# Another place for a block's attention steps in the first tile of a fused attention and two-layer network kernel

## The chip, the cores and the metric

The kernel runs on one core of a Trainium2 chip. The metric is the device time of one execution, in microseconds. Before the change it is 1495.19 us (median of 3 runs, 1493.69 to 1496.91). The execution that was profiled took 1492.79 us; its span in the trace is 1491.0 us.

## The reference

Attention is computed in chunks of 64 positions (softmax of 0.125 * q k^T over 64 keys, times v) for 8 batches, 8 heads and 576 positions, head size 64. Its output is reshaped to 4608 tokens of 512 numbers. Then come two networks:

```
attn = softmax(0.125 * q_c @ k_c.T)          # per chunk of 64, rows divided by (sum + 1e-9)
x = (attn @ v_c) as 4608 x 512
h = x @ w_in                                 # 512 -> 2048
x = (h * cos(h)) @ w_out                     # 2048 -> 512
y = ((x @ w1) * (x @ w2)) @ w3 @ moe2_w_out  # 512 -> 1024, 1024 -> 1024, 1024 -> 512
```

All is in float32. On TensorE each operand is split into a high part and a low part, and each product is made of three matmuls (`mm3`: high*high on L107, high*low on L108, low*high on L109).

## The kernel before

The 4608 tokens are worked in 9 tiles of 512 tokens. A tile's attention is done in 4 blocks of 128 tokens. The first network runs in two passes over the tiles. The first pass does groups 0 to 4 of the 8 groups into which w_in and w_out are cut, the second does groups 5 to 7. The change is in the first pass over tile 0, that is, in the first five groups (i = 0 to 4), which are the only ones that use the strings `ORDER0` (groups 0 to 3) and `ORDER0E` (group 4).

The work is written out by hand: the loop at L823 walks the string of its group letter by letter, and each letter emits instructions at the end of the queues of the engines. Every engine then works through its own queue in that order. What the letters do in these groups:

- `P` and `Q`: the **first product** and the **second product** of the group, each two blocks of 12 matmuls of 256 columns into one of two PSUM buffers (`bank_h`). The first block needs the group's first w_in part in W, the second block the second one. A buffer comes free when `B` (for P) or `D` (for Q) of the group before has read it.
- `s`: the product of the group before is split into high (ScalarE, L598) and low (GpSimd, L599) parts, two instructions each.
- `x` and `y`: the first and the second half of the **output product** of the group before (24 matmuls of 512 columns in all).
- `a`, `A`, `b`, `B` and `c`, `C`, `d`, `D`: the chain from h to h * cos(h) for P and for Q. The small letter is ScalarE's (L576, then the sine at L586), the capital one VectorE's (L581, then the product at L590).
- `v`: one step of the conversion of the weights (`conv_tick`, L189); there are four in a group, called **steps 1 to 4** here. A step does its part for three weights at once. On ScalarE: L183 (high part), L130, and L206 for w_out. On VectorE: L138, L131, L132, and L209 (low part) for w_in. For w_out the low part is added by a transfer that GpSimd issues (L207, w<-cw). Steps 1 and 2 finish the two w_out parts of the group; steps 3 and 4 finish the two w_in parts of the next group.
- `q`: the next attention step of the group's block, in the order **scores** (L386 on TensorE, then two maxima and two subtractions on VectorE, L395 and L397, and the loads of a coming q and k block), **exponential** (ScalarE, L403), **scale** (sums and reciprocals on VectorE, L408 to L411, then a multiplication on GpSimd, L412), **transposes** (TensorE, L419, then a copy on ScalarE, L422) and **values** (TensorE, L433, two copies on ScalarE, L438, and the load of the next v block).

Sine and exponential are in different ScalarE tables, so an `ACT_TABLE_LOAD` stands before the one that follows the other.

In a group before the change the scores stand between P and Q, the exponential behind Q and step 2, the scale behind C, the transposes behind D, and the values at the very end. Block 4 + n is done within group n, for n = 0 to 3. Group 4 has no attention steps. It splits tile 1's input (`o`, L477: a high part on ScalarE and a low part on VectorE, four times), which group 5's first product needs.

Of the kernel before, what the change touches and what calls it, by code (L numbers as in the profile page):

```python
# [34 lines left out]
START = "A0 A1 B0 x B1 E0 A2 C0 B2 E1 A3 D0 C1 x B3 D1 E2 o o E3 C2 D2 x C3 D3 x o o"  # L35
NE = 4

ORDER0 = "PsvaAqQvqcCqxybBdvDqvq"
ORDER0E = "PsvaAQvcCxybBodDoooL"
ORDER1P = "PsqMhQqqHaclAxqbCrRmBdyqDL"  # L40
ORDER1PE = "SPsQacATCoobBoxodoDyoo"
ORDER1 = "1s2qMh5qqHa3clAxqbCrRmBdyqDL"
# [15 lines left out]
def chunk_attention_two_ffn(  # L58
# [38 lines left out]
    def f32(ap):  # L97
        return ap.bitcast(F32)
# [119 lines left out]
    def sum_load(g):  # L218
        pair = ("in", g)
        loaded.append((g, pair, new_w((pair, 2))))  # L220
        nc.sync.dma_start(out=f32(W[pair, 2]), in_=wr[g])
# [23 lines left out]
    def need(*keys):  # L245
        while not all(key in W for key in keys):
            assert (pump() if cat[3] == len(cq) else conv_tick()), keys
# [4 lines left out]
    def st_load():  # L252
        while sat[0] < min(len(sq), sat[2] + 2):
            load_w(sq[sat[0]])
            sat[0] += 1
# [40 lines left out]
    def st_hi():  # L296
        for _, x, hi, lo in now.get("parts", ()):
            nc.scalar.activation(hi.bitcast(F32R), x, AF.Copy)
# [143 lines left out]
    def att_tok(step, early):  # L442
        (att_scores, att_softmax, att_scale, att_transpose, att_values)["ABECD".index(step[0])](int(step[1:]), early)
# [144 lines left out]
    def chain_g(i, h, which):  # L588
        t = rr[i, which]
        nc.vector.tensor_tensor(out=t, in0=t, in1=h, op=ALU.mult)  # L590

    def split_g(i):

        gg[i] = t = one.tile([P, 8, 256], F32R, tag="g", name="g")
        for which in range(2):
            r = rr.pop((i, which)).rearrange("p (i t) -> p i t", i=2)
            hi, lo = (t[:, 2 * s + which:2 * s + which + (6, 4)[which]:(5, 3)[which]] for s in range(2))
            nc.scalar.activation(hi, r, AF.Copy)  # L598
            nc.gpsimd.tensor_tensor(out=lo, in0=r, in1=f32(hi), op=ALU.subtract)  # L599
# [44 lines left out]
    def load_w3():  # L644
        key = ("w3", n3[0])
        n3[0] += 1
        if key in staged:
            W[key] = t = wk.tile([P, 2, TT], F32R, tag="qk", name="w3")
            nc.sync.dma_start(out=f32(t), in_=staged.pop(key))
# [134 lines left out]
    with tc.manual_schedule():  # L784
# [22 lines left out]
        def order_of(i, nth, end):  # L807
            if i < GA:
                return ORDER0E if end else ORDER0
            if i < 2 * GA:  # L810
                return ORDER1PE if end else ORDER1P
            if i <= iA:
                return ORDER1E if end else ORDER1
            if i < iB:
                return ORDER2
            return (ORDER3X if nxt in xs else ORDER3E) if end else ORDER3B if nth else ORDER3
# [3 lines left out]
        iA, iB = (NTILE - 1) * GA, NTILE * GA  # L820
        n_sums = 0
        fq = 0
        for i in range(NG):  # L823
            if i == GA:
                sq.extend(("wo2", j) for j in range(FB2))
                for g in range(GA, G1):
                    sq.extend((nm, 2 * g + e) for nm in ("in", "out") for e in range(2))
                    lq.extend((("in", g), p_) for p_ in range(4))
                    lq.extend(("out", 2 * g + e) for e in range(2))
                lq.extend(("wo2", j) for j in range(FB2))  # L830
                sq.extend(("w3", j) for j in range(N3))
                for f in range(FB2):
                    sq.extend((nm, f) for nm in ("w1", "w2"))
                    if N3 + f < 16:
                        sq.append(("w3", N3 + f))
                lq.extend((("w12", u), p_) for u in range(UNITS) for p_ in range(4))
                st_load()
            if i == iB + FOLD - 1:
                load_w3()
                load_w3()  # L840
            ps, n, g = groups[i]
            k_tile = (i - iB) // (G1 - GA)
            nxt = PASS2[k_tile + 1] if 0 <= k_tile < NTILE - 1 else None
            nth = (g, g - GA)[ps]
            end = g == (GA, G1)[ps] - 1

            def load_x(op):
                if op in pre:
                    X[op], pre[op] = pre[op], X[op]
                else:  # L850
                    nc.sync.dma_start(out=f32(X[op]), in_=xs[nxt][op])

            need(*((("in", g), p_) for p_ in range(2 if i < 2 * GA else 4)))
            z = Plain(("in", g)) if i < 2 * GA else Seven(
                ("in", g), (bank_h,) * 4, False, load_x if ps and end and nxt in xs else None)
            if i:
                need(*(("out", 2 * groups[i - 1][2] + e) for e in range(2)))
            n_q = n_o = 0
            for op in order_of(i, nth, end):
                if op == "s" and i:  # L860
                    split_g(i - 1)
                elif op == "x" and i:
                    x2_mm(i - 1, 0)
                elif op == "y" and i:
                    x2_mm(i - 1, 1)
                elif op == "v":
                    conv_tick()
                elif op == "L":
                    if n_sums < GA:
                        sum_load(n_sums)  # L870
                        n_sums += 1
                elif op == "M":
                    if loaded and i > GA + loaded[0][0]:
                        sum_make()
                elif op in "HR":
                    if sp:
                        {"H": sum_hi, "R": sum_lo}[op]()
                elif op == "l":
                    st_low()
                elif op == "m":  # L880
                    st_bits()
                elif op == "h":
                    st_hi()
                elif op == "r":
                    st_lo()
                elif op in "1253PQ":
                    getattr(z, "step" + op)()
                elif op in "ac":
                    chain_t(i, z.d if op == "a" else z.e, "ac".index(op))
                elif op in "AC":  # L890
                    chain_r(i, z.d if op == "A" else z.e, "AC".index(op))
                elif op in "bd":
                    chain_cos(i, "bd".index(op))
                elif op in "BD":
                    chain_g(i, z.d if op == "B" else z.e, "BD".index(op))
                elif op == "q":
                    if i < iA and nth < 4:
                        att_tok(steps[20 * n + 5 * nth + n_q], False)
                    elif i >= iB + FOLD and fq < 4 * FB2:
                        need(("w3", fq // 2), *(("wo2", j) for j in range(FB2)))  # L900
                        fold(fq // 4, fq % 4)
                        fq += 1
                        if fq == 4 * FB2:
                            load_wf(0)
                            load_wf(1)
                    n_q += 1
                elif op in "ST":
                    x_sums("ST".index(op))
                elif op == "o":
                    if i < GA and not n_o:  # L910
                        x_plain()
                    x_op((z.done if i < GA or i >= 2 * GA else OPS)[n_o], n + 1 if ps == 0 else None)
                    n_o += 1
            if i >= iA:
                pump()
            if n == (NTILE - 1, PASS2[-1])[ps]:
                done_with((("in", g), p_) for p_ in range(4))
            if ps == 1:
                if nth == 0 and nxt in xs:
                    if not pre:  # L920
                        xr = one.tile([P, CC, TT], F32R, tag="xf", name="xr")
                        pre.update((op, xr[:, 2 * j:2 * j + 2]) for j, op in enumerate(("B11", "B21")))
                    for op in pre:
                        nc.sync.dma_start(out=f32(pre[op]), in_=xs[nxt][op])
                if nth == 0 and nxt not in xs:
                    if pre:
                        pre.clear()
                        xf = one.tile([P, CC, TT], F32, tag="xf", name="xf")
                    nc.sync.dma_start(out=xf, in_=x2d[ALONE] if nxt is None else xd[nxt])
                if end:  # L930
                    for c in range(CC):
                        load_x2a(n, c)
# [119 lines left out]
```

## Time and profile before

| | before |
|---|---|
| median of 3 runs | 1495.19 us |
| profiled execution / its span | 1492.79 / 1491.0 us |
| TensorE matmul busy | 1447.5 us, 97% |
| VectorE busy | 1089.2 us, 73% |
| ScalarE busy | 692.0 us, 46% |
| GpSimd busy | 272.7 us, 18% |

The busy shares are means over all stages. The span is cut in 40 slices of 37.3 us on the page: TensorE is busy for 6 and 7 tenths in the first two and for nine or more in nearly all others. The first tile lies between 27.6 and 108.6 us. A view of busy times by stretch gives for each stretch its length and the busy time of TensorE's matmuls (PE), its weight loads (PEld), VectorE (DVE), ScalarE (ACT) and GpSimd (POOL), each with its count of instructions, and the granted TensorE clock as a share of 2.4 GHz. The stretches below begin and end where a group's first product ends: in groups 0, 1, 2, 3 and 4 at 32.9, 50.4, 69.6, 84.1 and 100.4 us; at 108.6 us the first product of group 5 begins. A row of a timeline tells when an instruction started, how long it took, its engine, line and operands, and in brackets how long its engine had been idle and what released it. A count such as x2 means that as many neighbours were merged. An instruction can start before the row ahead of it has ended, since the engines overlap the end of one with the start of the next.

### The profile page before, as it was taken

To read this page: it belongs to the slowest core of one execution; us is meant where nothing else is said; L and a number is where in the kernel's file an instruction comes from. 1 tells how busy PE (TensorE), PEld (TensorE's weight loads), DVE (VectorE), ACT (ScalarE), POOL (GpSimd) and SP (SyncE) were. 2 spreads that over 40 slices of the span, in tenths; PEclk is the share of its full clock that TensorE was granted. 3 is DMA by queue.
4 is the path that set the end of the run, shared out by engine and by line. 5 is a ranking of instruction groups with operands and counts; after the bars stand their busy time and mean duration, and the time that the engine had idled before them with its cause. 6 is when DMAs were issued, how large, how long until landed. Compare 5 with 4: busy or idle time off the path is not lost.

```text
span 1491.0 us, 26050 instructions
## 1 busy us (share of the span) xinstructions
PE 1447.5 (97%) x9996; PEld 1251.0 (84%) x9996; DVE 1089.2 (73%) x1834; ACT 692.0 (46%) x1183; POOL 272.7 (18%) x204
## 2 busy tenths in 40 slices
PE   6799999999999999999999999999999999999998
PEld 5688888888888889988888889998888888888887
DVE  7886788898888887777777777676565666656553
ACT  4776677787776775444444444231032023014002
POOL 0332222222222222221122222122000100200000
PEclk9899999999999999999999999999999999999999
DMA  8784656575664718998889784586435442641611
GB/s 270 216 243 143 217 174 217 163 244 192 220 226 139 247 65 297 372 335 323 303 309 333 241 294 148 193 332 247 148 113 192 169 148 96 234 150 58 212 35 57
DMA packets 124252, 310.00 MB, mean 208 GB/s; under 512 B 13792, under 2 KB 25824, under 8 KB 122976
## 3 DMA queue, kind: packets, MB, share of 16 engines
q1 hardware_dynamic: 122688, 305.71, 58.9%
q0 software_dynamic: 1440, 2.62, 1.0%
q8 instruction: 79, 1.29, 0.4%
q14 instruction: 45, 0.37, 0.1%
HBM read 210.50 MB, written 95.16 MB: 205 GB/s over the span
## 4 chain that ended last, share of the span: by engine, by line
PE 77%; DVE 10%; ACT 5%; DMA 3%; issue 2%; POOL 2%; SPq 0%; DVEq 0%; ACTq 0%; POOLq 0%
PE acc L107 11%; PE acc L108 11%; PE acc L109 10%; PE ps_hh L107 10%; PE ps_hh L109 10%; PE ps_hh L108 10%; PE ps_aa L107 5%; PE ps_aa L108 5%; PE ps_aa L109 5%; ACT L403 2%; POOL ex L412 1%; DMA w<-cw 1%; DVE sm L408 1%; PE ps_at L419 1%; PE ps_v L433 1%
## 5 line engine op out<-in xcount | busy, mean ns | idle before, releaser
L599 POOL TENSOR_TENSOR g<-t,g 128x512 fp32r<-128x512 f32 x144 | 198.4, 1398 | 559.2 <-ACT g L598 504.7
L107 PE MATMUL acc<-g,w 128*128 128x512 f32 x576 | 228.6, 397 | 0.0
L108 PE MATMUL acc<-g,w 128*128 128x512 f32 x576 | 226.1, 392 | 0.0
L109 PE MATMUL acc<-g,w 128*128 128x512 f32 x576 | 225.0, 391 | 0.0
L109 PE MATMUL ps_hh<-T,w 128*128 128x256 f32 (+1 forms) x616 | 182.5, 296 | 5.0 <-DVE w L209 5.0
L107 PE MATMUL ps_hh<-T,w 128*128 128x256 f32 (+1 forms) x616 | 185.2, 301 | 0.0
L108 PE MATMUL ps_hh<-T,w 128*128 128x256 f32 (+1 forms) x616 | 182.0, 295 | 0.0
L109 PEld LDWEIGHTS acc<-g,w 128*128 128x128 f32 x576 | 108.6, 189 | 23.6
L109 PEld LDWEIGHTS ps_hh<-T,w 128*128 128x128 f32 x616 | 118.8, 193 | 8.1 <-DVE w L209 5.6
L108 PEld LDWEIGHTS acc<-g,w 128*128 128x128 f32 x576 | 109.0, 189 | 19.8 <-POOL g L599 0.6
L107 PEld LDWEIGHTS acc<-g,w 128*128 128x128 f32 x576 | 109.0, 189 | 19.8
L107 PE MATMUL ps_hh<-B,w 128*128 128x256 f32 (+1 forms) x396 | 120.6, 304 | 4.0 <-DVE t L590 2.6
L107 PEld LDWEIGHTS ps_hh<-T,w 128*128 128x128 f32 x616 | 118.7, 193 | 5.4
L108 PEld LDWEIGHTS ps_hh<-T,w 128*128 128x128 f32 x616 | 118.8, 193 | 3.2
L109 PE MATMUL ps_hh<-B,w 128*128 128x256 f32 (+1 forms) x396 | 116.9, 295 | 0.2 <-DVE w L209 0.2
L108 PE MATMUL ps_hh<-B,w 128*128 128x256 f32 (+1 forms) x396 | 116.9, 295 | 0.0
L773 ACT ACTIVATE phl<-e 128x512 fp32r<-128x512 f32 x32 | 20.3, 633 | 202.0 <-DVE e L771 202.0
L586 ACT ACTIVATE t<-t,half_pi 128x512 f32<-128x512 f32 x144 | 98.4, 716 | 1.4
L107 PE MATMUL acc<-wf,phl 128*128 128x512 f32 x252 | 98.2, 390 | 0.0
L108 PE MATMUL acc<-wf,phl 128*128 128x512 f32 x252 | 98.1, 389 | 0.0
L109 PE MATMUL acc<-wf,phl 128*128 128x512 f32 x252 | 98.0, 389 | 0.0
L576 ACT ACTIVATE t<-d 128x512 int32<-128x512 f32 x62 | 38.9, 627 | 121.3 <-DVE d L530 121.3
(211 smaller groups left out, 3431.5 us busy)
## 6 DMA issues: line engine op xcount, KB each, us to landing
w<-sd SPq DMA_DIRECT2D x159, 512.0 KB, 6.0
sd<-raw SPq DMA_DIRECT2D x104, 256.0 KB, 4.5
s<-sd SPq DMA_DIRECT2D x43, 256.0 KB, 5.1
qk<-in_q_dram SPq DMA_DIRECT2D x36, 256.0 KB, 4.5
qk<-in_k_dram SPq DMA_DIRECT2D x36, 256.0 KB, 4.6
x2a<-x2o SPq DMA_DIRECT2D x36, 256.0 KB, 3.1
x2a<-x2a SPq DMA_DIRECT2D x36, 256.0 KB, 5.6
x2d<-x2a SPq DMA_DIRECT2D x36, 256.0 KB, 3.1
```

The costliest lines, as they stand in the source:

```text
L107: nc.tensor.matmul(ps, a[0], b[0], start=first, stop=False)
L108: nc.tensor.matmul(ps, a[0], b[1], start=False, stop=False)
L109: nc.tensor.matmul(ps, a[1], b[0], start=False, stop=last)
L403: nc.scalar.activation(ex, ex, AF.Exp, scale=SCALE)
L408: nc.vector.reduce_sum(out=sm, in_=ex, axis=AX.X)
L412: (nc.vector if early else nc.gpsimd).tensor_tensor(out=ex, in0=ex, in1=rc.unsqueeze(2).to_broadcast([P, 2 * HP, 64]), op=ALU.mult)
L419: nc.tensor.transpose(ps[:, P * h:P * h + P], ex[:, 2 * h:2 * h + 2].rearrange("p e k -> p (e k)"), ident)
L433: nc.tensor.matmul(ps[c][64 * e:64 * e + 64, h], vt[r, e, h], pt[r, h, o:o + 64], start=True, stop=True)
L576: nc.scalar.activation(t.bitcast(I32), h, AF.Copy, scale=INV2PI, bias=0.25)
L586: nc.scalar.activation(t, t, AF.Sin, scale=TWO_PI, bias=half_pi)
L599: nc.gpsimd.tensor_tensor(out=lo, in0=r, in1=f32(hi), op=ALU.subtract)
L773: nc.scalar.activation(t[:, 0], e0, AF.Copy)
```

## The change

The four `q` of `ORDER0` go, and digits take their places: 6 scores, 7 exponential, 8 scale, 9 transposes, 0 values. The digits 6, 7 and 8 work on the group's own block, 9 and 0 on the block of the group before, so that they do nothing in group 0. Group 4 gets 9 and 0 for the last block of the tile.

```
-ORDER0 = "PsvaAqQvqcCqxybBdvDqvq"
-ORDER0E = "PsvaAQvcCxybBodDoooL"
+ORDER0 = "PsvaA9Qv0cCx6ybBd7vD8v"
+ORDER0E = "PsvaA9Qv0cCxybBodDoooL"
...
+        at_first = {c: NE for c in "67890"}
...
+                elif op in "67890":
+                    if i or op in "678":
+                        att_tok("ABECD"["67890".index(op)] + str(at_first[op]), False)
+                        at_first[op] += 1
```

So the transposes stand between P and Q (where the scores stood), the values behind Q and step 2, the scores between x and y, the exponential behind the second sine (`d`), and the scale between D and step 4.

## Rows read from the trace of the kernel before

**Rows 1.** Busy times by stretch: from:to, us, five engines, clock, DMA share, GB/s
```profile
32.90:50.40 17.50, 11.46 (x121) 10.31 (x120) 14.80 (x25) 12.06 (x21) 5.83 (x5) 0.71 0.72 212
50.40:69.60 19.20, 15.06 (x145) 13.04 (x145) 15.57 (x26) 13.23 (x22) 5.65 (x5) 0.93 0.83 222
69.60:84.10 14.50, 13.81 (x145) 12.30 (x144) 12.92 (x24) 12.82 (x22) 3.50 (x3) 0.97 0.77 244
84.10:100.40 16.30, 13.86 (x144) 12.27 (x144) 16.09 (x25) 12.92 (x23) 7.99 (x8) 1.00 0.82 242
100.40:108.60 8.20, 8.20 (x50) 7.24 (x49) 5.07 (x9) 5.53 (x10) 1.18 (x2) 1.00 1.02 287
108.60:1491.00 1382.40, 1366.24 (x9117) 1179.76 (x9115) 1001.06 (x1675) 619.88 (x1057) 246.91 (x176) 1.00 0.59 205
```

**Rows 2.** Timeline of TensorE, groups 0 to 2
```profile
42.07 1.12 PE L419 MATMUL ps_at<-ident,ex 128*128 128x128 f32 x4 [5.35 <-POOL ex L412]
...
48.27 0.58 PE L109 MATMUL ps_hh<-T,w 128*128 128x256 f32 x1
...
50.37 0.69 PE L386 MATMUL ps_s<-qk 64*64 64x64 f32 x32
51.00 0.39 PE L107 MATMUL ps_hh<-T,w 128*128 128x256 f32 x1
...
53.98 0.40 PE L107 MATMUL acc<-g,w 128*128 128x512 f32 x1
...
59.45 0.60 PE L419 MATMUL ps_at<-ident,ex 128*128 128x128 f32 x4
60.73 0.79 PE L433 MATMUL ps_v<-pt,vt 64*64 64x64 f32 x32 [0.69 <-ACT pt L422]
...
67.11 0.58 PE L109 MATMUL ps_hh<-T,w 128*128 128x256 f32 x1 [3.23 <-DVE w L209]
...
69.54 1.06 PE L386 MATMUL ps_s<-qk 64*64 64x64 f32 x32
```

**Rows 3.** Timeline of VectorE, groups 0 and 1
```profile
38.01 0.43 DVE L131 TENSOR_SCALAR cw<-raw 128x512 uint32<-128x512 uint32 x1 [1.70 <-DMA w<-cw]
...
51.77 0.75 DVE L395 TENSOR_REDUCE mx<-ps_s 128x4 f32<-128x256 f32 x2
52.44 0.75 DVE L397 TENSOR_TENSOR ex<-ps_s,mx 128x256 f32<-128x256 f32 x2
...
55.79 0.67 DVE L408 TENSOR_REDUCE sm<-ex 128x8 f32<-128x512 f32 x1
...
57.22 0.69 DVE L590 TENSOR_TENSOR t<-t,ps_hh 128x512 f32<-128x512 f32 x1 [0.31 <-ACT t L586]
...
60.38 0.43 DVE L131 TENSOR_SCALAR cw<-raw 128x512 uint32<-128x512 uint32 x1 [1.70 <-issue]
...
63.70 1.68 DVE L132 SCALAR_TENSOR_TENSOR cw<-raw,cw 128x512 uint32<-128x512 uint32 x1
65.31 1.75 DVE L209 TENSOR_TENSOR w<-cw,w 128x512 fp32r<-128x512 f32 x1
```

**Rows 4.** Timeline of GpSimd, group 1 and the start of group 2
```profile
57.09 1.04 POOL L412 TENSOR_TENSOR ex<-ex,rc 128x512 f32<-128x512 f32 x1 [3.21 <-DVE rc L411]
63.56 2.94 POOL L599 TENSOR_TENSOR g<-t,g 128x512 fp32r<-128x512 f32 x2 [5.44 <-ACT g L598]
```

**Rows 5.** Timeline of ScalarE, group 1 and the start of group 2
```profile
54.58 0.58 ACT L576 ACTIVATE t<-ps_hh 128x512 int32<-128x512 f32 x1
55.17 1.28 ACT L586 ACT_TABLE_LOAD   x1
56.46 1.34 ACT L586 ACTIVATE t<-t,half_pi 128x512 f32<-128x512 f32 x2
...
62.27 0.64 ACT L438 ACTIVATE xf<-ps_v 128x256 f32<-128x256 f32 x2
```

**Rows 6.** The page's transfer issues, KB each, median us from issue to landing
```profile
qk<-in_q_dram SPq DMA_DIRECT2D x36, 256.0 KB, 4.5
```

## The prediction

> **What bounds the kernel now.** Read the busy times by stretch first. Behind the first tile TensorE is busy for 1366.24 of 1382.40 us [rows 1]: nothing there can take back or give much, so what the first tile gains or loses goes into the total nearly one to one. From the end of group 0's first product to that of group 4's pass 17.5 + 19.2 + 14.5 + 16.3 = 67.5 us, of which TensorE is busy for 11.5, 15.1, 13.8 and 13.9 us [rows 1]. So TensorE waits here; VectorE is busy for 14.8, 15.6, 12.9 and 16.1 us, and in group 3 to 4 that is all but 0.2 us of the stretch. The timeline of TensorE shows for what it waits. In group 0 it idles 5.35 us before the transposes, for GpSimd's scale; before each values it idles 0.69 us, for ScalarE's copy; in group 2 it idles 3.23 us within the first product, for VectorE's L209, the low part of the second weight [rows 2]. The last is the one that sets the pace. The second block of a first product can't run until step 4 of the group before has made that low part, and step 4 stands behind all else on VectorE's queue.
>
> The timeline of VectorE shows this queue and two things that stretch it. Its L131 waits for a buffer that a transfer of w_out still reads (until 38.01 in group 0, until 60.38 in group 1, 10.0 us after the first product's end at 50.37) [rows 2, 3]. And while GpSimd splits (2.94 us) VectorE slows: L132 and L209 take 1.61 and 1.75 us, where the six instructions from 60.38 to 63.70 took 0.55 us on the mean [rows 3, 4]. That is 3.36 - 1.10 = 2.26 us lost in one split.
>
> **The change part by part.** It adds no work but ScalarE's table loads. It takes away the 5.35 us and the 0.69 us waits on TensorE: the copy of the transposes gets the second product as cover, and the values come behind it. But it makes one chain out of two. Before, scores, maxima and subtractions ran while the second product ran; now the scores come behind transposes, second product, values and the first half of the output product. VectorE takes its queue in order, so the waiting maxima hold back g (L590), step 3, the other g, the scale and step 4, and TensorE waits for step 4. I follow a group from T, the end of its first product, to the next one's.
>
> - TensorE to the end of the scores: transposes 0.60, second product 53.98 - 51.00 = 2.98, values 0.79, half of the output product (59.45 - 53.98) / 2 = 2.73, scores 51.00 - 50.37 = 0.63 [rows 2]. Sum 7.7; the transposes come right behind a wait, and at the lower clock such a group of four took 1.12 instead of 0.60 [rows 2], so I take 8.0. The other way to the maxima is shorter: values end at 4.4, copies 0.64, ScalarE's first step of the chain 0.58 [rows 5], VectorE's about 0.6: 6.2. VectorE stands idle between.
> - Maxima and subtractions: two pairs, 0.67 apart [rows 3]: 1.33, now 9.3.
> - g, step 3 (L138, L131, L132, L209), g: six instructions, 3.4 by the run of six above [rows 3]: 12.7. L131's transfer wait ends at about 10.0 + 0.6 (transposes' copy ahead of it on ScalarE) = 10.6, and VectorE gets there at 10.5: 0 to 0.4, I take 0.
> - Scale on VectorE: sums and reciprocals, 1.30 until GpSimd begins (55.79 to 57.09) [rows 3, 4], VectorE itself 1.1: 13.8.
> - Step 4: four instructions, 2.2. GpSimd now multiplies (1.04) and then splits (2.94) just in this time, since the split's inputs are ready at 13.7, and step 4 has no other place. Without any overlap 2.2; with both in full 2.2 + 2.26 + 0.8 (in proportion) = 5.3. I take the split in full and half of the other: 4.9, so 18.7.
> - Rest of the first product: ten matmuls, 69.54 - 67.11 = 2.43 after the 3.23 us wait, at 1.2 GHz [rows 2]; at 2.4 GHz half, 1.2. TensorE is done with the rest of its work at about 11 and with the first block at 13, so it idles 5 us before it, more than the 3.23: I take 2.4. The next T is at 21.1.
>
> So 21 us a group. Groups 1 to 4 (three such steps) take 63 instead of 19.2 + 14.5 + 16.3 = 50.0: **+13.0**. VectorE gives a check: 16.1 us of busy time in group 3 to 4 [rows 1] and some 3 us of idle time before the first step's end and 1.5 before the maxima make 20.6.
>
> Group 0 has nothing of the block before and no output product. VectorE waits until 38.01 as before, for the same transfer [rows 3]. From there: L131 and L132 1.1, C 0.6, maxima and subtractions 1.33 (in the wait before, now behind it), 3.4, 1.1, 4.9: step 4 ends at 50.4, where TensorE got it at 48.27 [rows 2]. TensorE saves its 5.35 us and waits as long for weights. **+2.4** with the rounding of the lower clock (bounds 0 and 3).
>
> Group 4 gains transposes and values on TensorE: 0.60 + 2.98 + 0.79 + 5.47 + 0.3 = 10.1 to group 5 instead of 8.2 [rows 1, 2]: **+1.9**. Its sine needs a table load again (1.28 [rows 5]); values' copies, chain, load, sine and the split of the first input end at some 9, hidden by the output product.
>
> ScalarE's loads (two each in groups 0 to 3, one in group 4, two more than before) cost 1.28 each [rows 5]: load, two sines 1.34, load and exponential end at about 10, the subtractions at 9.3, and the exponential is first needed at 12.7: hidden, and if not, up to 1.3 a group. The moved transfers: the q and k loads now wait for scores 8 us later and stand ahead of step 3's weight load, which is emitted after them; they land in 4.5 us [rows 6] and are needed a group later; the v load likewise: 0, and below a group's slack no price.
>
> Sum: 13.0 + 2.4 + 1.9 = 17.3 us. The profiled execution took 1492.79 us, so 1510 by it; it lies 2.4 under the median of 1495.19, and the timed median should become 1495.2 + 17 = **1512 us**.
>
> One rule speaks for more. The lost 2.26 us stand against 2.94 us of split [rows 3, 4], so VectorE got something done in between. The Trainium skill, SBUF — State Buffer, section "SBUF: two separate sides", says that the port pair that VectorE and GpSimd share is locked for a whole instruction and the loser stands still. By it step 4 would take 2.2 + 3.98 = 6.2 instead of 4.9, and the time would be some 5 us longer, 1517.
>
> **The rivals.** (a) The overlap with GpSimd falls elsewhere (the split comes later than step 4) and the clock stays up: 21.1 - 2.7 - 1.2 = 17.2 a group, +1.6 for three, group 0 at 0, group 4 +1.9: +3.5 to +8 if half of it comes true, 1499 to 1503. For it: before, half of the split fell on the next group's step 1, where it cost nothing. Against it: the scale now stands right ahead of step 4. (b) The lower clock lasts on through second product and values: 1.5 to 3 more a group, 1516 to 1521. For it: stretches at 0.71 and 0.93 [rows 1] followed idle times of 5.35 and 3.23. (c) Faster: VectorE isn't what decides, TensorE's sum does, and the groups all take the 14.5 of group 2 to 3: 4 x 14.5 - 67.5 = -9.5, with group 4's +1.9 a time of 1488. It decides if the maxima find their scores before VectorE reaches them, at 6.2 after T; by the rows they come at 8. Against it also: 16.09 busy in 16.30. (d) The waits only change places and the first tile stays within 3 us, if group 1's transfer wait (10.0 us) covers the whole wait for the scores and the split in step 4 costs as much as before.
>
> **How the numbers follow.** Forecast 64%, (a) 14%, (b) 13%, (c) 5%, (d) 4%. Range 1502 to 1520: from the upper part of (a) to the lower part of (b). Some 3 us, 0.2%, is what a measurement of this kernel can tell from no change. Faster 0.05, same 0.05, slower 0.90.
>
> **What would show it.** Right: TensorE without the 5.35 us wait before transposes, but with waits of 4 to 6 us for L209 in the second block of each first product of groups 1 to 4; the maxima waiting for the scores; L132 and L209 of step 4 at over 1.5 us beside GpSimd's split; stretches of 20 to 22 us; group 5 beginning at about 126. Wrong: groups under 17 us, the first product not waiting for L209, or a time that moves in the second tile or later.

## The result and the profile after

The changed kernel takes 1514.39 us (median of 4 runs, 1511.71 to 1516.0), the kernel before 1494.44 us in the same runs. The ratio is 1.0131, with a 95% interval of 1.0109 to 1.0154: slower, by 16 to 23 us. The profiled span went from 1491.0 to 1509.9 us; the profiled execution is the shortest of the four.

Busy times by stretch after, cut where first products end as in [rows 1] (length, then TensorE's matmuls, its weight loads, VectorE, ScalarE, GpSimd, the granted clock, DMA share, GB/s):

```profile
32.60:51.80 19.20, 9.50 (x81) 8.64 (x80) 15.42 (x25) 12.52 (x19) 6.12 (x6) 0.75 0.71 193
51.80:73.20 21.40, 15.30 (x142) 13.16 (x142) 15.50 (x25) 13.50 (x22) 6.03 (x5) 0.90 0.67 185
73.20:95.70 22.50, 16.38 (x141) 14.24 (x141) 15.51 (x25) 13.53 (x22) 6.04 (x5) 0.88 0.64 176
95.70:117.30 21.60, 15.49 (x141) 13.35 (x141) 14.46 (x23) 12.96 (x21) 6.02 (x5) 0.90 0.49 134
117.30:128.50 11.20, 11.20 (x87) 10.04 (x86) 3.64 (x6) 7.68 (x14) 0.85 (x1) 0.85 0.43 125
128.50:1509.90 1381.40, 1364.05 (x9117) 1177.51 (x9115) 1000.92 (x1678) 620.29 (x1058) 247.75 (x176) 1.00 0.59 206
```

The whole difference lies in the first tile. Against [rows 1] the stretches grew by 1.7, 2.2, 8.0, 5.3 and 3.0 us, and the rest of the kernel is 1.0 us shorter. VectorE's busy time did not grow with them (14.5 to 15.5 us); from group 1 on it idles for 6 to 7 us of each stretch, where before it idled for 0.2 to 3.6.

The timeline of TensorE after, groups 0 to 2 and the start of group 4:

```profile
41.79 0.58 PE L107 MATMUL ps_hh<-B,w 128*128 128x256 f32 x1 [5.73 <-ACT w L183]
...
49.48 0.58 PE L109 MATMUL ps_hh<-T,w 128*128 128x256 f32 x1 [3.80 <-DVE w L209]
...
51.79 0.95 PE L419 MATMUL ps_at<-ident,ex 128*128 128x128 f32 x4
...
55.53 0.69 PE L433 MATMUL ps_v<-pt,vt 64*64 64x64 f32 x32
...
59.10 0.69 PE L386 MATMUL ps_s<-qk 64*64 64x64 f32 x32
...
64.18 0.39 PE L109 MATMUL ps_hh<-B,w 128*128 128x256 f32 x1 [1.08 <-DVE w L209]
...
70.90 0.58 PE L109 MATMUL ps_hh<-T,w 128*128 128x256 f32 x1 [5.01 <-DVE w L209]
...
73.20 1.05 PE L419 MATMUL ps_at<-ident,ex 128*128 128x128 f32 x4
...
78.05 0.69 PE L433 MATMUL ps_v<-pt,vt 64*64 64x64 f32 x32
...
117.32 1.05 PE L419 MATMUL ps_at<-ident,ex 128*128 128x128 f32 x4
...
122.27 0.69 PE L433 MATMUL ps_v<-pt,vt 64*64 64x64 f32 x32
```

The waits for the scale (5.35) and for the copies (0.69) of [rows 2] are gone. In group 0 TensorE waits 5.73 us for weights in their place. In its second block the first product of group 1 waits 3.80 us for L209, and those of groups 2 to 4 wait 5.01 to 5.03 us, where the longest such wait was 3.23 us before.

VectorE in group 1 after, from the chain's C to the end of step 4:

```profile
57.46 0.69 DVE L581 SCALAR_TENSOR_TENSOR t<-ps_hh,t 128x512 f32<-128x512 f32 x1 [2.39 <-ACT t L576]
59.85 0.76 DVE L395 TENSOR_REDUCE mx<-ps_s 128x4 f32<-128x256 f32 x2 [1.70 <-PE ps_s L386]
60.52 0.74 DVE L397 TENSOR_TENSOR ex<-ps_s,mx 128x256 f32<-128x256 f32 x2
61.18 0.68 DVE L590 TENSOR_TENSOR t<-t,ps_hh 128x512 f32<-128x512 f32 x1
...
64.64 0.68 DVE L408 TENSOR_REDUCE sm<-ex 128x8 f32<-128x512 f32 x1
...
65.68 0.64 DVE L138 CUSTOM_DVE_ANT_0 cw<-raw,cw 128x1024 uint16<-128x1024 uint16 x1
66.24 1.27 DVE L131 TENSOR_SCALAR cw<-raw 128x512 uint32<-128x512 uint32 x1
67.54 1.64 DVE L132 SCALAR_TENSOR_TENSOR cw<-raw,cw 128x512 uint32<-128x512 uint32 x1
69.10 1.74 DVE L209 TENSOR_TENSOR w<-cw,w 128x512 fp32r<-128x512 f32 x1
70.77 0.68 DVE L138 CUSTOM_DVE_ANT_0 cw<-raw,cw 128x1024 uint16<-128x1024 uint16 x1
```

ScalarE between them, with the chain's first step, the sines and the exponential, each behind its table load:

```profile
56.82 0.61 ACT L576 ACTIVATE t<-ps_hh 128x512 int32<-128x512 f32 x1
57.45 1.28 ACT L586 ACT_TABLE_LOAD   x1
58.74 1.34 ACT L586 ACTIVATE t<-t,half_pi 128x512 f32<-128x512 f32 x2
60.09 1.28 ACT L403 ACT_TABLE_LOAD   x1
61.39 0.64 ACT L403 ACTIVATE ex<-ex 128x512 f32<-128x512 f32 x1
61.93 0.61 ACT L183 ACTIVATE w<-cw 128x512 fp32r<-128x512 f32 x1
```

GpSimd in the same time, the block's multiplication and then the two instructions of the split:

```profile
65.94 1.28 POOL L412 TENSOR_TENSOR ex<-ex,rc 128x512 f32<-128x512 f32 x1 [9.81 <-DVE rc L411]
67.19 3.11 POOL L599 TENSOR_TENSOR g<-t,g 128x512 fp32r<-128x512 f32 x2
```

Step 4 takes 70.77 - 65.68 = 5.1 us. Before, two of its four instructions were slowed [rows 3]; now it is three, beside both of GpSimd's works.

### The profile page after: what moved, and what is told of

Same layout as the page of the kernel before. It is cut to its first block, busy times and chain, and to the rows that moved or that the text cites. A ratio compares the mean times of both kernels' runs of the same rounds, so it can differ in the third digit from the quotient of the medians.

```text
span 1509.9 us, 26049 instructions
## 1 busy us (share of the span) xinstructions
PE 1449.9 (96%) x9996; PEld 1252.4 (83%) x9996; DVE 1089.1 (72%) x1834; ACT 695.9 (46%) x1185; POOL 274.4 (18%) x204
## 4 chain that ended last, share of the span: by engine, by line
PE 77%; DVE 11%; ACT 4%; DMA 4%; issue 2%; POOL 1%; SPq 0%; DVEq 0%; ACTq 0%; POOLq 0%
PE acc L107 10%; PE acc L108 10%; PE acc L109 10%; PE ps_hh L107 10%; PE ps_hh L109 10%; PE ps_hh L108 10%; PE ps_aa L107 5%; PE ps_aa L108 5%; PE ps_aa L109 5%; ACT L403 2%; POOL ex L412 1%; DVE sm L408 1%; DVE ex L397 1%; PE ps_at L419 1%; PE ps_v L433 1%
## 5 line engine op out<-in xcount | busy, mean ns | idle before, releaser
L109 PE MATMUL ps_hh<-T,w 128*128 128x256 f32 (+1 forms) x616 | 183.6, 298 | 18.9 <-DVE w L209 18.9
```

Source lines behind the costliest of these rows:

```text
L109: nc.tensor.matmul(ps, a[1], b[0], start=False, stop=last)
```

## The experiments

All ratios are to the kernel before, run beside each; 0.001 is 1.5 us. Unless told otherwise an experiment differs from the changed kernel in the strings alone. (It was five `q` that gave way to the five digits, not four as written above.) T is the end of a group's first product, as in the prediction.

**1. Scores back between the products.**

```diff
-ORDER0 = "PsvaA9Qv0cCx6ybBd7vD8v"
+ORDER0 = "PsvaA96Qv0cCxybBd7vD8v"
```

> Of the changed order only one thing is undone: the scores stand between the first and the second product again (behind the transposes); exponential, scale, transposes and values stay where the change put them. Theory S (the maxima on VectorE's queue wait for scores behind the output product's first half, and this is on the chain to step 4): the 1.7 us wait before the maxima and the 1.33 us of maxima and subtractions leave the chain, some 3 us in each of groups 1 to 3 and 1.3 in group 0, so 9 to 10 us less than the changed kernel, about 1505 us; L209 waits on TensorE stay, at some 3 us. Theory G (only VectorE's loss to GpSimd in step 4 counts): no change, 1514. Theory C (TensorE's own extra work between the products and its lower clock count): no change or slower.

Measured: 1.0159 (1.0137 to 1.0180), 1517.1 us. Not faster: theory S as it stood is refuted. VectorE of this run, in group 1 (T, the end of the first product, is 53.67):

```profile
56.19 0.76 DVE L395 TENSOR_REDUCE mx<-ps_s 128x4 f32<-128x256 f32 x2 [0.90 <-PE ps_s L386]
...
61.05 0.69 DVE L581 SCALAR_TENSOR_TENSOR t<-ps_hh,t 128x512 f32<-128x512 f32 x1 [1.79 <-ACT t L576]
...
63.09 0.69 DVE L590 TENSOR_TENSOR t<-t,ps_hh 128x512 f32<-128x512 f32 x1 [1.34 <-ACT t L586]
...
66.15 0.69 DVE L209 TENSOR_TENSOR w<-cw,w 128x512 fp32r<-128x512 f32 x1 [0.71 <-ACT w L183]
```

The maxima are off the way, and g (L590) still comes at 63.09 - 53.67 = 9.42 after T, as in the changed kernel (61.18 - 51.79 = 9.39). Now it waits for ScalarE's sine, and step 3's L209 waits 0.71 us for ScalarE's L183. In the changed kernel the first sine is done at 58.74 + 0.7 = 59.4, 7.7 after T, 1.7 us ahead of the subtractions. The scores, which now stand in front of the second product, wait for a PSUM buffer that the transposes' copy frees, and with them second product, values, copies, chain and sine come 1.7 us later:

```profile
55.41 0.73 PE L386 MATMUL ps_s<-qk 64*64 64x64 f32 x30 [0.28 <-ACT pt L422]
```

The clock takes part too: groups 2 and 3 last 24.5 and 24.2 us here (22.5 and 21.6 in the changed kernel), and from transposes to values the granted clock is 0.54 and 0.57 in them. So this run does not price the scores alone.

**2. Scale behind step 4.**

```diff
-ORDER0 = "PsvaA9Qv0cCx6ybBd7vD8v"
+ORDER0 = "PsvaA9Qv0cCx6ybBd7vDv8"
```

> The changed order with one exchange: the scale stands behind step 4 instead of ahead of it. Theory S with the changed kernel's rows: step 4 loses the 1.1 us of sums and reciprocals ahead of it, and as GpSimd takes its multiplication first and the split after it, both slide behind step 4, which then takes 2.3 instead of 5.1 us: 3.9 us a group, four groups, 15 to 16 us less than the changed kernel, about 1499. If GpSimd's overlap stays on step 4: only 1.1 a group, 1510. Theory C: no change, 1514.

Measured: 1.0060 (1.0039 to 1.0080), 1501.81 us: some 10.6 us less than the changed kernel, not 15 to 16. Step 4 does run free (L209 takes 0.68). But GpSimd issues a transfer of w_out behind the split, and this is now later, 52.59 us, 3.0 after T, where it was 48.83, 3.0 before T, in the changed kernel. L131 of step 3 waits 1.83 us. The row names no releaser (`issue`), so that it waits for this transfer is argued from group 0, where the row names it [rows 3]. In two groups TensorE also waits some 1 us for the scale before the transposes.

```profile
61.80 0.43 DVE L131 TENSOR_SCALAR cw<-raw 128x512 uint32<-128x512 uint32 x1 [1.83 <-issue]
...
65.73 0.68 DVE L209 TENSOR_TENSOR w<-cw,w 128x512 fp32r<-128x512 f32 x1
```

**3. Both.**

```diff
-ORDER0 = "PsvaA9Qv0cCx6ybBd7vD8v"
+ORDER0 = "PsvaA96Qv0cCxybBd7vDv8"
```

> Scores back between the products and scale behind step 4; transposes and values stay in the next group. If the two terms add (10 + 16): 1488 to 1490, under the kernel before. If the transfer of w_out (VectorE's L131 free some 10 us after the first product's end) takes over as the bound of a group: step 4 ends at 10.6 + 4.6, groups of 16 to 17 us, 1493 to 1497, no different from the kernel before, and VectorE shows waits for the transfer or for issue ahead of L131.

Measured: 1.0079 (1.0062 to 1.0097), 1505.73 us. Neither expectation holds. As in experiment 1 the scores' return gave nothing (experiment 2 has 1.0060).

**4. The split's low part on VectorE** in groups 0 to 3, the order as changed.

```diff
-            nc.gpsimd.tensor_tensor(out=lo, in0=r, in1=f32(hi), op=ALU.subtract)
+            (nc.vector if i < 4 else nc.gpsimd).tensor_tensor(out=lo, in0=r, in1=f32(hi), op=ALU.subtract)
```

> The changed order as it is, but in groups 0 to 3 the low part of the split (L599) is made on VectorE, behind step 4 in its queue, instead of on GpSimd. It measures GpSimd's price alone. By the rows of the changed kernel step 4 takes 5.1 us beside GpSimd's multiplication and split; without the split some 2.9: 2.3 us less in each of four groups, and the two low parts (1.2 us) come behind L209 where VectorE waits anyway: about 9 us less, 1505. Theory S alone, with the contention costing nothing: 1514 or, with 1.2 us more on VectorE, 1516 and above.

Measured: 1.0074 (1.0053 to 1.0096), 1504.29 us: 8.5 us less than the changed kernel by the ratios, 9 expected. GpSimd's split beside step 4 is a cause, and not the only one.

**5. Transposes and values alone in the next group**; scores, exponential and scale where they were before the change.

```diff
-ORDER0 = "PsvaA9Qv0cCx6ybBd7vD8v"
+ORDER0 = "PsvaA96Qv70cC8xybBdvDv"
```

> One half of the change alone: transposes and values stand in the next group, between the products and behind the second one; scores, exponential and scale stand where the kernel before had them (scores between the products, exponential behind step 2, scale behind C). Theory S+G (a group is one chain from T, the end of a first product, over the maxima or over values' copies, chain and sine, to g, step 3, scale, step 4; the loss is the later g and GpSimd beside step 4): the scale is ahead of g as before, so GpSimd's split comes later than most of step 4; g at about T + 8.4 where the kernel before has 6.9 and the changed one 9.4; step 4 done at about 14 to 15; groups of 16 to 17.5 as before. 1493 to 1499. Rival L (moving transposes and values into the next group is itself the loss, since they delay the second product's chain): 1504 and above.

Measured: 1.0091 (1.0076 to 1.0106), 1506.19 us. I had expected 1493 to 1499; rival L's number came out. VectorE of this run, group 1 (T is 51.15):

```profile
58.70 0.69 DVE L581 SCALAR_TENSOR_TENSOR t<-ps_hh,t 128x512 f32<-128x512 f32 x1 [1.79 <-ACT t L576]
...
60.73 0.69 DVE L590 TENSOR_TENSOR t<-t,ps_hh 128x512 f32<-128x512 f32 x1 [0.31 <-ACT t L586]
...
64.37 1.60 DVE L138 CUSTOM_DVE_ANT_0 cw<-raw,cw 128x1024 uint16<-128x1024 uint16 x1
65.90 1.49 DVE L131 TENSOR_SCALAR cw<-raw 128x512 uint32<-128x512 uint32 x1
```

Two things are to be seen. g comes 60.73 - 51.15 = 9.6 after T, where it came 57.22 - 50.37 = 6.9 after it before [rows 2, 3]. And step 4 is slowed though the scale is ahead of g: GpSimd's split now begins ahead of step 4's first instruction:

```profile
64.13 2.98 POOL L599 TENSOR_TENSOR g<-t,g 128x512 fp32r<-128x512 f32 x2 [2.49 <-ACT g L598]
```

Its high parts begin on ScalarE 1 us ahead of step 4, directly behind the sine and the work for the weights:

```profile
63.38 0.62 ACT L598 ACTIVATE g<-t 128x512 fp32r<-128x512 f32 x1
```

Before, the copies of transposes and values, with a wait of 1.21 us for the transposes, stood ahead of the high parts on ScalarE, which began 0.15 us behind step 4's start (62.65):

```profile
60.08 0.60 ACT L422 ACTIVATE pt<-ps_at 128x512 f32<-128x512 f32 x1 [1.21 <-PE ps_at L419]
...
62.80 1.15 ACT L598 ACTIVATE g<-t 128x512 fp32r<-128x512 f32 x2
```

So the split began with step 4's third instruction (63.56 and 63.70) [rows 3, 4]. In the old order these copies held GpSimd off half of step 4; experiment 10 puts this to the test.

**6. That half with the split on VectorE.**

```diff
-ORDER0 = "PsvaA9Qv0cCx6ybBd7vD8v"
+ORDER0 = "PsvaA96Qv70cC8xybBdvDv"
...
-            nc.gpsimd.tensor_tensor(out=lo, in0=r, in1=f32(hi), op=ALU.subtract)
+            (nc.vector if i < 4 else nc.gpsimd).tensor_tensor(out=lo, in0=r, in1=f32(hi), op=ALU.subtract)
```

> e4 (transposes and values alone in the next group) with the split's low part on VectorE in groups 0 to 3. In e4 GpSimd's split fell in full on L138 and L131 of step 4 (1.60 and 1.49 us for 0.60 and 0.45), since ScalarE's copies of transposes and values no longer stand ahead of the split's high parts. Theory G2 (the late half costs two things: a chain that begins 2.7 us later, behind transposes and values, and the split that slides onto step 4): 2 us less in each of four groups, 8 in all, 1498 us. Rival (the later chain alone is the cost and VectorE is not the bound there): 1505 to 1507.

Measured: 1.0000 (0.9986 to 1.0013), 1492.93 us: 13.6 us less than experiment 5, more than the 8 expected. Step 4 runs free, the split follows it:

```profile
65.25 0.68 DVE L209 TENSOR_TENSOR w<-cw,w 128x512 fp32r<-128x512 f32 x1
65.86 1.28 DVE L599 TENSOR_TENSOR g<-t,g 128x512 fp32r<-128x512 f32 x2
```

TensorE's wait for this L209 went from 3.17 us in experiment 5

```profile
68.78 0.39 PE L109 MATMUL ps_hh<-T,w 128*128 128x256 f32 x1 [3.17 <-DVE w L209]
```

to 1.16 us here,

```profile
65.99 0.39 PE L109 MATMUL ps_hh<-T,w 128*128 128x256 f32 x1 [1.16 <-DVE w L209]
```

and the group from 70.08 - 51.15 = 18.9 to 67.28 - 50.98 = 16.3 us.

**7. The kernel before with the split on VectorE** (against that kernel):

```diff
-            nc.gpsimd.tensor_tensor(out=lo, in0=r, in1=f32(hi), op=ALU.subtract)
+            (nc.vector if i < 4 else nc.gpsimd).tensor_tensor(out=lo, in0=r, in1=f32(hi), op=ALU.subtract)
```

> The kernel before, but in groups 0 to 3 the low part of the split (L599) is made on VectorE instead of GpSimd: the price of GpSimd's split in the old order. There half of it fell on step 4 (1.1 us) and half on the next group's step 1. If the price is as in the changed kernel (2.1 us a group) 8 us less, 1486; by theory, as VectorE now does 1.2 us more itself and only the half on step 4 was on the chain, 0 to 4 us less, 1490 to 1494.

Measured: 0.9983 (0.9971 to 0.9995), 1489.42 us: some 2.5 us less than before by the ratio, as theory had it. It beats both kernels.

**8. The other half alone**: scores, exponential and scale where the change has them, transposes and values at the end of their own group.

```diff
-ORDER0 = "PsvaA9Qv0cCx6ybBd7vD8v"
-ORDER0E = "PsvaA9Qv0cCxybBodDoooL"
+ORDER0 = "PsvaAQvcCx6ybBd7vD8v90"
+ORDER0E = "PsvaAQvcCxybBodDoooL"
...
-                    if i or op in "678":
+                    if True:
```

> The other half of the change alone: scores between the output product's halves, exponential behind the second sine, scale ahead of step 4; transposes and values at the end of the block's own group as before the change. TensorE then waits at the end of the group for the scale (some 14 us after T) and for the copy before it may begin the next first product. Theory A+G2: g comes at T + 8, step 4 in full beside GpSimd's multiplication, transposes at 15, values at 16.5, the whole first product behind them: groups of 19 to 20 us, 1506 to 1512. If only the moved transposes and values cost (e4's 12 to 14 us): 1492 to 1496.

Measured: 1.0118 (1.0093 to 1.0143), 1511.49 us, at the upper end of what was expected. The groups were not: T at 53.3, 76.1, 97.9 and 120.3 makes 21.8 to 22.8 us each, not 19 to 20. TensorE of this run waits at the end of each group, for the scale and then for the copy, and the first product behind these waits begins at a granted clock of 0.50 (70.8 to 73.7):

```profile
68.01 1.12 PE L419 MATMUL ps_at<-ident,ex 128*128 128x128 f32 x4 [5.36 <-POOL ex L412]
69.81 1.23 PE L433 MATMUL ps_v<-pt,vt 64*64 64x64 f32 x32 [0.69 <-ACT pt L422]
```

**9. Shorter ways to g, the scale still ahead of step 4.** First the values behind C:

```diff
-ORDER0 = "PsvaA9Qv0cCx6ybBd7vD8v"
+ORDER0 = "PsvaA9QvcC0x6ybBd7vD8v"
```

> The changed order with the values emitted directly behind C instead of ahead of c: on TensorE nothing moves, on ScalarE the chain's first step no longer stands behind the values' copies, so only the arm over the sine gets shorter, by some 0.6 us. Theory A: the arm over the maxima still ends at T + 9.4: no change, 1513 to 1515. If the sine's arm alone decides: 2 to 3 us less, 1511.

Measured: 1.0152 (1.0132 to 1.0172), 1514.31 us: no change, as theory A has it. Then scores back and the values behind step 3:

```diff
-ORDER0 = "PsvaA9Qv0cCx6ybBd7vD8v"
+ORDER0 = "PsvaA96QvcCxybBd7v0D8v"
```

> The changed order with scores back between the products and values moved behind step 3 (TensorE does them after the output product); the scale stays ahead of step 4. New theory A after the first experiments: g waits at T + 9.4 for two arms of the same length, scores to maxima (transposes, second product, values, half output product, scores, maxima) and values to sine (transposes, second product, values, copies, chain, table load, sine). The scores moved back lengthened the second arm by as much as the first had led. With both arms shortened g comes at about T + 7.6; L131 in step 3 then waits for the transfer of w_out (issued 3.6 after T, free 5.7 to 7.4 later), so that 0.5 to 2 us of a group are gained: 5 to 7 less than the changed kernel, about 1508. If the arms don't matter (only GpSimd beside step 4 does): 1514 to 1517.

Measured: 1.0153 (1.0126 to 1.0180), 1513.24 us: a miss. VectorE of that run, group 1 (T is 53.80):

```profile
62.06 0.69 DVE L590 TENSOR_TENSOR t<-t,ps_hh 128x512 f32<-128x512 f32 x1 [1.35 <-ACT t L586]
...
65.12 0.69 DVE L209 TENSOR_TENSOR w<-cw,w 128x512 fp32r<-128x512 f32 x1 [0.71 <-ACT w L183]
```

g does come earlier, at 8.3 after T, but then step 3's L209 waits for ScalarE's L183, which stands behind the exponential and its table load. L209 begins 11.3 after T, in the changed kernel 63.44 - 51.79 = 11.65 after it. A third way leaves only 0.35 us of the gain. The first two groups show it (21.1 us each, 21.4 and 22.5 in the changed kernel); the third lasts 23.5 us, with a granted clock of 0.50 from 97.0 to 102.5, so that nothing is left.

**10. The late half with its prices taken off one by one.** Values behind step 3:

```diff
-ORDER0 = "PsvaA9Qv0cCx6ybBd7vD8v"
+ORDER0 = "PsvaA96Qv7cC8xybBdv0Dv"
```

> e4 with the values emitted behind step 3 instead of behind step 2: they and their copies leave the way to the second product's chain, and the copies stand ahead of the split's high parts again. Theory G2: the chain begins 1.4 us earlier and the sine with it; L131 of step 3 still waits for the transfer of w_out, so 0 to 1.6 us a group are gained there, and 1 us a group from the split that comes later: 3 to 8 us less than e4, 1498 to 1503. Rival (any place of the block's steps in the next group costs as much): 1505 to 1507.

Measured: 1.0035 (1.0014 to 1.0055), 1498.8 us, as expected: 8 us less than experiment 5 by the ratios. With the values' copies ahead of the split's high parts again the split comes later. In group 1 it begins when step 4 is all but done and runs beside the next group's step 1. The end of step 4 on VectorE:

```profile
65.07 0.69 DVE L209 TENSOR_TENSOR w<-cw,w 128x512 fp32r<-128x512 f32 x1
```

The split on GpSimd:

```profile
65.53 3.05 POOL L599 TENSOR_TENSOR g<-t,g 128x512 fp32r<-128x512 f32 x2 [4.86 <-ACT g L598]
```

The ten runs spread from 1492 to 1505 us, and the profiled one's groups last 15.8, 20.1 and 18.0 us. In the second of them the split begins at step 4's second instruction and slows it. With the split on VectorE too:

```diff
-            nc.gpsimd.tensor_tensor(out=lo, in0=r, in1=f32(hi), op=ALU.subtract)
+            (nc.vector if i < 4 else nc.gpsimd).tensor_tensor(out=lo, in0=r, in1=f32(hi), op=ALU.subtract)
```

> e10 with the split's low part on VectorE in groups 0 to 3: the half change with both of its prices taken off. If G2 is the whole story it is level with the kernel before with the same split (1489.4), but for the 1.9 us that group 4's transposes and values cost: 1490 to 1495. If something else of the later block costs: 1497 and above.

Measured: 0.9995 (0.9981 to 1.0008), 1492.57 us, as expected, and no different from the kernel before.

A table of the halves (ratio to the kernel before):

| order | split on GpSimd | split on VectorE |
|---|---|---|
| before | 1 | 0.9983 |
| transposes and values moved | 1.0091 | 1.0000 |
| scores, exponential and scale moved | 1.0118 | not run |
| all moved (the change) | 1.0131 | 1.0074 |

The halves do not add: either alone costs most of what both cost together.

## Why the prediction was right

**The time.** 1512 was forecast, with +17.3 us; the median is 1514.39, 20.0 us above the kernel before in the same runs, and the span grew by 18.9. By its terms: three groups at 65.5 us instead of 50.0, +15.5 (forecast +13.0); group 0, from 32.6 instead of 32.9, 19.2 instead of 17.5, +1.7 (+2.4); group 4 +3.0 (+1.9); the rest of the kernel with its start -1.3 (0). So the sum is nearer than its terms, and that is luck: some 3.6 us too little in groups 1 to 4 stand against 2.0 too much elsewhere, and 1.3 of these lie where the change does nothing.

**The walk through a group** holds at each of its points in group 1 after, counted from T = 51.79: scores end at 8.0 (forecast 8.0), the subtractions at 9.4 (9.3), step 3's L131 starts at 10.6 without a wait (10.5), second g at 12.85 (12.7), the scale's part on VectorE at 13.9 (13.8), step 4 at 19.0 (18.7), the next T at 21.4 (21.1). Of the signs that were named, group 1's wait for L209 (3.80) and the stretches of groups 0 and 2 (19.2 and 22.5) lie just outside, and group 5 begins at 128.5 instead of 126.

**What was too small** is the lower clock. In group 2, behind the 5 us wait, the transposes and the first eleven of the second product's 24 matmuls ran at 1.2 GHz (granted clock 0.50 from 73.2 to 76.2): from transposes to values it is 78.05 - 73.20 = 4.85 us there, and 55.53 - 51.79 = 3.74 in group 1, where the clock was 1.00 from 52.6 on. That is 1.1 of group 2's 22.5 us. In group 4 it is 122.27 - 117.32 = 4.95 us at a granted clock of 0.65, 1.2 more than in group 1, which is all that this term lay above the forecast. Rival (b) was true in part.

**What was wrong is a reason, not the sum.** The prediction put the loss on the scores ("the waiting maxima hold back g"), and so it is in the changed kernel. But it wrote "The other way to the maxima is shorter", ending that way at 6.2, with VectorE's C. That C did come at 6.3, but the two ways join at g, which needs the sine, and behind the chain's first step stand a table load of 1.28 us and the first sine: that way ended at 7.7, not 6.2, against 9.4 for the maxima's. So the scores hold g back by 1.7 us at most, and experiment 1 shows what this means: with the maxima out of the way g comes at the same time, since the scores only moved to the other way. Nor had the table loads the room that was written. The exponential was to be needed only at 12.7, but behind it on ScalarE stands an L183 that step 3's L209 needs: it ends at 61.93 + 0.61 = 62.5, and L209 starts at 63.44, so the room was 0.9 us. In experiments 1 and 9 L209 does wait for it. Three ways of nearly one length lead to step 3, and shortening one or two gave nothing, in part because the clock fell in some of their groups.

**Step 4 beside GpSimd** was priced at 4.9 us and took 5.1. By its cause the prediction saw half. It named the scale ahead of step 4; experiment 5 shows that moving transposes and values alone brings the split onto step 4, because their copies no longer delay it on ScalarE, and experiment 10 shows it leaving again with the values' copies put back ahead of it. That half of the change costs 13.6 us with the split on GpSimd and 2.5 with the split on VectorE (experiment 6 against experiment 7), so some 11 us of it are the split's place. In the profiled runs 2.0 us in each of three groups are TensorE's shorter wait for L209, and 1.5 are group 4 (11.1 and 9.6 us), where the clock no longer falls: 4.90 and 3.41 us from transposes to values, at granted clocks of 0.66 and 1.00. The rest is not separated. In the full change the same edit returns 8.5 us. The remaining 11 us (1.0074) go when scores, exponential and scale return too (1.0000). How they divide among these three is open: the scores' return alone gave nothing, the scale's alone 10.6 us, part of it GpSimd's. These three moved alone cost 17.6 us too (experiment 8), but by another wait, for the scale at the end of the group; with the split on VectorE that half was not run.

The Trainium skill, SBUF — State Buffer, section "SBUF: two separate sides", has the loser of the shared ports stand still for a whole instruction, for VectorE's instructions in a 2-port mode or with two inputs in SBUF. By the prediction's estimate from that, step 4 was to take 6.2 us. Step 4 took 5.1 us beside 1.28 + 3.11 = 4.4 us of GpSimd's work, 2.8 more than the 2.27 that it takes free in experiment 6 (63.59 to 65.86): the forecast 2.7 rather than the estimate's 4.0. The measurement decides on the estimate, which charged VectorE with all of GpSimd's durations, but not on the rule. Three of VectorE's instructions stretch to 1.27, 1.64 and 1.74 us, by 0.85 to 1.06 each, one for each of GpSimd's three instructions, and L138, which began ahead of them, is not slowed. If the two engines take turns by instruction, GpSimd's durations hold waits of their own (1.28 for a multiplication that took 1.04 before), and the loss comes out smaller than their sum. No run tells this from a sharing within an instruction.

**Rivals.** (a) fell: the overlap with GpSimd lies on step 4 in full and the clock does drop. (c) and (d) fell: TensorE's sum doesn't decide, and the first tile grew by far more than 3 us, though in group 0 the wait did only change places (5.35 us for the scale, 5.73 for weights).

## What to carry to other kernels

Follow a loop from one point round to the same point of the next turn, over all engines, before moving a step in it: a wait that disappears from the busiest engine may have been covered anyway, and the step that caused it comes back in the loop at another place. Follow each way to a join up to the join itself (here g and step 3, not C): where several are of one length, undoing one shows little, and a table of halves tells more. Ask of each step that is moved what it held off where it stood; here the copies of transposes and values on ScalarE kept GpSimd from running beside VectorE's most urgent instructions.

## What the runs showed of the hardware

GpSimd too pays for the overlap: its multiplication takes 1.28 us beside step 4 and 1.04 before [rows 4]. The two instructions of the split take 1.28 us on VectorE and 2.94 to 3.11 on GpSimd, so that VectorE is ahead by doing them itself: beside them it lost some 2 us (64.37 to 67.43 for two instructions in experiment 5 that take 63.59 to 64.64 in experiment 6). After a table load the next ScalarE instruction starts at once (55.17 + 1.28 = 56.45, and 56.46) [rows 5].
